# Loads behind the first K issued by GpSimd, one packet per engine and load, in an attention decode kernel

## The chip, the cores and the metric

The kernel runs on one core of a Trainium2 chip. Its engines are TensorE (PE in the profile), VectorE (DVE), ScalarE (ACT), GpSimd (POOL) and SyncE (SP); 16 DMA engines move data between HBM and the on-chip memory of 128 partitions. An engine puts a transfer on a DMA queue with one instruction, and a semaphore tells when it has landed. The metric is the device time of one execution in microseconds (us). Before the change it is 1299.59 us, the median of three runs (1299.52 to 1299.6).

## The reference

One decode step: attention of one query over a cache of 8192 keys, for 2 batches and 32 heads of size 128, times a gate that a small MLP computes, plus the input. Everything is fp32.

```python
x = A_x                                   # (2, 1, 512)
xn = _layernorm(x, axis=-1)
q = (xn @ wq).reshape(B, Sq, H, Dh) ...   # to (2, 32, 1, 128)
scores = jnp.einsum("bhqd,bhkd->bhqk", q, k_cache) * (Dh ** -0.5)
p = _softmax(scores, axis=-1)
o = jnp.einsum("bhqk,bhkd->bhqd", p, v_cache)
s = o ... @ wo                            # (4096, 512)
y = _layernorm(xn); h = _gelu(y @ w1 + b1)
g = _silu(h @ w2 + b2)
return x + s * g
```

The two caches have 2 x 32 x 8192 x 128 elements each, 268 MB each. With the weights the kernel reads 559 MB, each byte once.

## The kernel before

**Tiling.** A unit of work is two heads of one batch, so there are N = 32 units. For each unit the K cache is one load of 128 partitions with 64 KB each (partitions 0 to 63 hold one head, 64 to 127 the other; a partition holds 128 keys of 128 elements), and so is the V cache. On chip there are two buffers for K, `kb[0]` and `kb[1]`, used in turn, and one for V, `vb`. The first and last K and the last V are loaded in two halves of 32 KB per partition.

**Start-up.** `vb` first holds the MLP's weights and small tiles, and `kb[0]` holds wq. SyncE issues w1, w2, the two biases, wq and both halves of the first K (unit 0, into `kb[1]`) without a wait. The MLP runs first; then PE multiplies by wq (line 481), ScalarE copies q, and PE and ScalarE spread q over the partitions (lines 494 and 496). K of unit 1 goes into `kb[0]`, so its load waits for PE's last read of wq; V of unit 0 goes into `vb`, so its load waits for the last reader of the MLP's tiles.

**Loop.** For unit n VectorE multiplies K with q in two halves, in place (line 523), sums each half over the 128 elements into the scores (line 530), and takes the maximum (line 534). Its order within unit n is: multiply first half, maximum of unit n-1 across partitions (line 540), multiply second half, sum first half, sum second half, maximum. PE and ScalarE then do the softmax of unit n-1 (lines 546 to 555), PE multiplies with V (line 574), ScalarE copies the result (line 581). A load of K for unit n+2 is issued when VectorE has summed unit n, whose buffer it overwrites; a load of V for unit n is issued when PE has finished with unit n-1, as there is one V buffer. The last V goes in halves into `kb[1]`. In the end wo is loaded into `vb` in five pieces, and PE multiplies the attention output with it (lines 647 and 656).

**Order.** Every operation is recorded first (`Plan.op`) with the tiles that it reads and writes; `Plan.emit` gives each engine its operations in the order of recording and puts before each the semaphore waits that follow from these tiles. An engine works through its list in order, so a load that waits holds back all that stands behind it on the issuing engine. All loads go through the function `load` at line 313; before the change all of them are SyncE's (line 314). GpSimd has no work after the start-up's fills (lines 342 to 346).

Of the kernel before, what the change touches and what calls it, by code (L numbers as in the profile page):

```python
# [21 lines left out]
class Plan:  # L22
# [18 lines left out]
    def op(self, eng, fn, r=(), w=(), over=(), it=None, loop=False, dma=None):  # L41


        o = Op()
        o.eng, o.fn, o.it, o.loop, o.dma, o.tell = eng, fn, it, loop, dma, False
        need = {}

        def after(d, war):
            if d.dma is None and dma is None and d.eng == eng and (eng == "pe" or war):
                return  # L50
            if d.dma is None:
                if need.get(d.eng) is None or need[d.eng].idx < d.idx:
                    need[d.eng] = d
            else:
                k = ("dma", d.dma)
                if need.get(k) is None or need[k].idx < d.idx:
                    need[k] = d

        for k in r:
            if k in self.writer:  # L60
                after(self.writer[k], False)
        for k in list(w) + list(over):
            if k in self.writer:
                after(self.writer[k], False)
            for d in self.readers.get(k, ()):
                after(d, True)
        clock = self.clock[eng]
        need = {k: d for k, d in need.items() if clock.get(k, 0) < d.idx}
        o.deps = [(k, d) for k, d in need.items()
                  if not any(e is not d and e.done.get(k, 0) >= d.idx for e in need.values())]  # L70
        for _, d in o.deps:
            for k, v in d.done.items():
                clock[k] = max(clock.get(k, 0), v)
        own = eng if dma is None else ("dma", dma)
        self.count[own] = o.idx = self.count.get(own, 0) + 1
        o.done = dict(clock)
        o.done[own] = o.idx
        for k in w:
            self.writer[k] = o
            self.readers[k] = []  # L80
        for k in r:
            if k not in w:
                self.readers.setdefault(k, []).append(o)
        self.ops.append(o)
# [80 lines left out]
def decode_kernel(nc, x, kc, vc, wq, wo, w1, b1, w2, b2, out):  # L165
# [31 lines left out]
    op = plan.op  # L197
# [112 lines left out]
    vf = vc.rearrange("b h s d -> (b h s d)").rearrange("(n p j d) -> n p j d", p=P, j=KP, d=DH)  # L310
    M = KP // 2

    def load(dst, src, sem, w, over=()):
        op("sp", lambda: nc.sync.dma_start(dst, src), (), w, over=over, dma=sem)  # L314

    def load_k(n):
        i = (n + 1) % 2
        if n in (0, N - 1):
            for s in range(2):
                load(kbuf[i][:, s * M:(s + 1) * M], kf[n][:, s * M:(s + 1) * M], f"k{i}{s}", [("kb", i, s)])  # L320
            return
        load(kbuf[i], kf[n], f"kb{i}", [("kb", i, s) for s in range(2)])
# [4 lines left out]


    load(w1_sb, w1.rearrange("(p c) f -> p c f", p=P), "w1", ["w1"])
    load(w2_sb, w2.rearrange("f n -> (f n)").rearrange("(p e) -> p e", p=P), "w2", ["w2"])  # L330
    for t, src, k in ((b1_sb, b1, "b1"), (b2_sb, b2, "b2")):
# [166 lines left out]


    PT, PM, PN = (t for t in scratch[:3])  # L500
    load_k(1)

    def load_v(n):
# [192 lines left out]
```

## Time and profile before

| | |
|---|---|
| median of the runs | 1299.59 us |
| span of the profiled execution | 1298.3 us |
| VectorE busy | 1134.7 us (87%) |
| PE busy | 409.4 us (32%) |
| ScalarE busy | 77.6 us (6%) |
| GpSimd busy | 1.4 us |
| DMA packets, bytes, mean rate | 10827, 559.39 MB, 431 GB/s |

The times of runs are of the whole execution on the device; the profiled execution has a span, from its first to its last instruction, which is 1.3 us less than the median of the runs. The profile lists the busy time of each engine, the span in 40 equal slices with the busy share of each engine and of the DMA engines in tenths, the DMA queues with their packets, the chain of work that ended last, and for each group of loads the time from its issue to its landing. The unit of one slice is 32.5 us. The order of time shows one row per instruction or group: its start, its length, engine, line, operation, tiles, and in brackets the idle time before it and what ended it.

### The profile page before, as it was taken

The page shows a single profiled execution, that of the slowest core. Times are in us where ns is not written, and L with a number is a line of the kernel's source. Part 1 is how long each engine was busy: PE and PEld are TensorE (multiplying, and loading weights), DVE is VectorE, ACT ScalarE, POOL GpSimd, SP SyncE. Part 2 cuts the span into 40 slices and gives each one's busy share as a digit, 9 for nine tenths or more (in the row PEclk, how much of TensorE's full clock was granted, in tenths as well). Part 3 has the DMA queues.
Part 4 walks back from the last instruction along what each step waited for, and adds up shares of the span by engine and source line. Part 5 has one row for each costly group of instructions (what it writes and reads, how often), then busy time and mean ns, then how long its engine had stood idle before and what let it go on. Part 6 is the DMA issues. An engine that isn't in the chain of part 4 may idle for free.

```text
span 1298.3 us, 6788 instructions
## 1 busy us (share of the span) xinstructions
PE 409.4 (32%) x2728; PEld 124.5 (10%) x2728; DVE 1134.7 (87%) x276; ACT 77.6 (6%) x250; POOL 1.4 (0%) x8
## 2 busy tenths in 40 slices
PE   5502333212333311333321333321333321333337
PEld 1100011000101000101100101000101100001103
DVE  3599989888889988889988888988888988888991
ACT  1100000000000000000000000000000000000000
POOL 0000000000000000000000000000000000000000
PEclk9856666556666556666555666655666655666659
DMA  9999999999999999999999999999999999999998
GB/s 406 445 423 444 424 436 436 426 444 426 440 428 430 440 426 444 424 436 436 426 444 426 440 428 434 438 424 444 426 434 436 426 444 426 440 428 434 423 436 360
DMA packets 10827, 559.39 MB, mean 431 GB/s; under 512 B 1208, under 2 KB 1216, under 8 KB 1476
## 3 DMA queue, kind: packets, MB, share of 16 engines
q1 hardware_dynamic: 10816, 559.30, 99.7%
q8 instruction: 4, 0.07, 0.0%
q14 instruction: 3, 0.02, 0.0%
q10 hardware_dynamic: 4, 0.00, 0.0%
HBM read 559.30 MB, written 0.00 MB: 431 GB/s over the span
## 4 chain that ended last, share of the span: by engine, by line
DMA 73%; PE 25%; DVE 1%; issue 0%; ACT 0%; SPq 0%; DVEq 0%
DMA vb<-in_A_v_cache_dram 71%; PE po L574 22%; DMA vb<-in_A_wo_dram 2%; PE s L409 1%; PE po L481 1%; PE s L451 0%; PE s L411 0%; PE acc L656 0%; DVE vb L417 0%; ACT L430 0%; DVE vb L355 0%; PE s L458 0%; SPq L314 0%; DVE vb L366 0%; DVE vb L443 0%
## 5 line engine op out<-in xcount | busy, mean ns | idle before, releaser
L523 DVE TENSOR_TENSOR kb<-kb,Q 128x8192 f32<-128x8192 f32 x64 | 555.6, 8681 | 106.3 <-DMA kb<-in_A_k_cache_dram 97.1
L530 DVE TENSOR_REDUCE sc<-kb 128x64 f32<-128x8192 f32 x64 | 552.3, 8666 | 0.0
L574 PE MATMUL po<-vb,PZ 128*8 128x512 f32 x1984 | 287.3, 744 | 296.4 <-DMA vb<-in_A_v_cache_dram 296.4
L546 PE MATMUL s<-nm,srow 1*128 1x2 f32 x64 | 18.4, 355 | 365.2 <-DVE nm L540 365.2
L574 PEld LDWEIGHTS po<-vb,PZ 128*8 128x8 f32 x1984 | 57.5, 104 | 500.2 <-issue 497.5
L537 PE MATMUL s<-ident,mx 128*1 128x128 f32 x32 | 11.8, 369 | 182.6 <-DVE mx L534 182.6
L546 PEld LDWEIGHTS s<-nm,srow 1*128 1x128 f32 x64 | 15.7, 302 | 374.5 <-DVE nm L540 374.5
L581 ACT COPY o<-po 128x512 f32<-128x512 f32 x32 | 18.7, 585 | 542.9 <-PE po L574 542.9
L547 ACT COPY bias<-s 128x2 f32<-128x2 f32 x32 | 5.1, 160 | 612.9 <-PE s L546 612.9
L583 PE MATMUL s<-mod,o 128*128 128x2 f32 x256 | 33.6, 253 | 22.1 <-ACT o L581 22.1
L583 PEld LDWEIGHTS s<-mod,o 128*128 128x128 f32 x256 | 31.1, 191 | 51.3 <-ACT o L581 51.3
L551 ACT ACTIVATE PZ<-sc,bias 64x128 f32<-64x128 f32 x64 | 25.5, 399 | 1.8
L537 PEld LDWEIGHTS s<-ident,mx 128*1 128x1 f32 x32 | 2.5, 79 | 186.1 <-DVE mx L534 155.5
L589 DVE TENSOR_TENSOR Z<-blk,s 128x8 f32 (+1 forms) x32 | 5.2, 163 | 12.4 <-PE s L583 12.4
L417 DVE COPY vb<-vb 2x384 f32<-2x384 f32 x4 | 1.8, 500 | 15.1 <-ACT vb L413 15.1
L551 ACT ACTIVATION_READ_ACCUMULATOR PZ<-sc,bias 64x1 f32 x64 | 11.8, 185 | 0.0
L409 PE MATMUL s<-vb 128*2 128x512 f32 (+1 forms) x24 | 11.7, 637 | 0.3 <-ACT vb L374 0.3
L665 DVE TENSOR_TENSOR gate<-acc,gate 128x128 f32<-128x128 f32 x1 | 0.3, 292 | 13.0 <-PE acc L656 13.0
L534 DVE TENSOR_REDUCE mx<-sc 128x1 f32<-128x128 f32 x32 | 9.2, 286 | 1.1
L555 ACT ACTIVATE ZR<-half,rs 128x8 f32 (+1 forms) x32 | 9.6, 301 | 4.1
L574 PE MATMUL po<-kb,PZ 128*8 128x512 f32 x64 | 8.7, 705 | 1.4 <-ACT PZ L551 1.4
L540 DVE TENSOR_REDUCE nm<-s 1x2 f32<-1x128 f32 x32 | 8.7, 272 | 0.3 <-PE s L537 0.3
(88 smaller groups left out, 83.8 us busy)
## 6 DMA issues: line engine op xcount, KB each, us to landing
kb<-in_A_k_cache_dram SPq DMA_DIRECT2D x4, 4096.0 KB, 43.3
kb<-in_A_v_cache_dram SPq DMA_DIRECT2D x2, 4096.0 KB, 40.5
vb<-in_B_w_dram SPq DMA_DIRECT2D x2, 2752.0 KB, 12.4
vb<-in_A_wo_dram SPq DMA_DIRECT2D x1, 4096.0 KB, 19.8
vb<-in_A_wo_dram SPq DMA_DIRECT2D x1, 2048.0 KB, 24.4
vb<-in_A_wo_dram SPq DMA_DIRECT2D x1, 1280.0 KB, 27.0
vb<-in_A_wo_dram SPq DMA_DIRECT2D x1, 512.0 KB, 27.7
vb<-in_A_v_cache_dram SPq DMA_DIRECT2D x31, 29.2
```

The lines of the kernel that those rows point to most:

```text
L409: pe(lambda f=f, w=w, ph=ph, c=c: matmul(ph[:B, :w], yT[:, c, :], w1_sb[:, c, f:f + w], start=(c == 0), stop=False), ["yT", "w1"], [k])
L481: pe(lambda i=i, c=c, wv=wv, a=a, j=j, hd=hd: matmul(PO[R * j:R * j + NQ * B, :].rearrange("m (h d) -> m h d", d=DH), xnT[:, c, a:a + NQ * ...
L523: vector(n, n, lambda n: nc.vector.tensor_tensor(out=k, in0=k, in1=cols(Q, n * DH, DH).unsqueeze(1).to_broadcast([P, M, DH]), op=ALU.mult) ...
L530: vector(n, n, lambda n: nc.vector.tensor_reduce(out=SC[:, s * M:(s + 1) * M], in_=k, axis=AX.X, op=ALU.add), [("kb", i, s)], [("sc", s)])
L534: vector(n, n, lambda n: nc.vector.tensor_reduce(out=MX, in_=SC, axis=AX.X, op=ALU.max), [("sc", 0), ("sc", 1)], ["mx"])
L537: pe(lambda i: transpose(PM[:1, :P], MX, ident), ["mx", "ident"], ["s1"], it=n, loop=n > 0)
L546: pe(lambda i: matmul(PN[:, :U], srow, NM, start=True, stop=True), ["srow", "nm"], ["s2"], **one)
L551: act(lambda i, r=r, s=s: nc.scalar.activation(PZ[r, :, s, :], sc[r], AF.Exp, bias=BIAS[r, s:s + 1], scale=SCALE, accum_out=RS[r]), ["bias ...
L555: act(lambda i: nc.scalar.activation(cols(ZR, i * UP - UP, UP), half, AF.Copy, scale=RS), ["half"] + [("rs", s) for s in range(U)], [("ZR" ...
L574: pe(lambda i, t=t, j=j, v=v: matmul(PO[R * j:R * j + U * JW, :], PZ[:, t].rearrange("p s j -> p (s j)"), v[:, t * JW:(t + 1) * JW, :].rea ...
L581: act(lambda i: nc.scalar.copy(O4, PO), ["po"], ["o4"], **one)
L583: pe(lambda i, k=k: matmul(PT[:, :U], O4[:, k * DH:(k + 1) * DH], mod[:, k:U * JW:JW], start=(k == 0), stop=(k == JW - 1)), ["o4", "mod"], ...
```

## The change

The function `load` gets a switch. It is off for the loads of the start-up (w1, w2, the biases, wq, both halves of the first K), which SyncE issues as before, and is turned on before the load of K for unit 1. [...] Waits, buffers, semaphores and the order of the loads among themselves are as before. The output is still stored by SyncE.

```diff
+    stream = [False]
+
     def load(dst, src, sem, w, over=()):
-        op("sp", lambda: nc.sync.dma_start(dst, src), (), w, over=over, dma=sem)
+        if stream[0]:
+            op("pool", lambda: nc.gpsimd.dma_start(dst, src, single_packet=True), (), w, over=over, dma=sem)
+        else:
+            op("sp", lambda: nc.sync.dma_start(dst, src), (), w, over=over, dma=sem)
...
     PT, PM, PN = (t for t in scratch[:3])
+    stream[0] = True
     load_k(1)
```

## The prediction

> **What bounds the kernel now.** I read first the engine totals and the DMA lines of the page, then the chain that ended last, then the order of time around the first issue that the change moves.
>
> ```profile
> span 1298.3 us, 6788 instructions
> DVE  3599989888889988889988888988888988888991
> DMA  9999999999999999999999999999999999999998
> DMA packets 10827, 559.39 MB, mean 431 GB/s; under 512 B 1208, under 2 KB 1216, under 8 KB 1476
> q1 hardware_dynamic: 10816, 559.30, 99.7%
> DMA 73%; PE 25%; DVE 1%; issue 0%; ACT 0%; SPq 0%; DVEq 0%
> kb<-in_A_k_cache_dram SPq DMA_DIRECT2D x30, 42.6
> vb<-in_A_v_cache_dram SPq DMA_DIRECT2D x31, 29.2
> ```
>
> The 16 DMA engines are busy from end to end, all on one queue (q1, SyncE's), and the chain is a transfer of V, PE's product with it, the next transfer of V. VectorE is nine tenths busy in the middle, so it has little room to catch up. The chain's period gives the pace of the loop:
>
> ```profile
> 45.66 49.55 DMA vb<-in_A_v_cache_dram
> 95.33 9.45 PE po L574 x64
> 104.79 29.11 DMA vb<-in_A_v_cache_dram
> 134.03 8.87 PE po L574 x64
> 142.92 29.69 DMA vb<-in_A_v_cache_dram
> 172.73 10.00 PE po L574 x64
> ...
> 1217.67 9.77 PE po L574 x64
> ```
>
> From 134.03 to 1217.67 are 28 rounds of 38.70 us, and one K and one V of 8.389 MB each in 38.70 us are 433.5 GB/s: 19.35 us for a load. A V takes 29.2 us from issue to landing, so it waits 9.8 us behind the K before it; a K (42.6) waits 23 us. What happens between an issue and its first byte is covered by these 9.8 and 23 us, as long as the queue is never empty. The time is set by the bytes and by any gap in the DMA.
>
> **The place where the change acts.** SyncE has put w1, w2, wq and both halves of the first K (K0) on its queue by 3.7 us. The next load, K1, must wait for PE's last read of wq. Here are the start-up's issues and landings, each landing row being the time since its issue, and then VectorE's and SyncE's order of time.
>
> ```profile
> L314 SPq DMA_DIRECT2D vb<-in_B_w_dram x1: 393/393/393, 0.7 to 0.7; - x1
> DMA to landing us min/median/max: 9.4/9.4/9.4
> ...
> L314 SPq DMA_DIRECT2D kb<-in_A_k_cache_dram x2: 457/466/474, 2.8 to 3.3; - x2
> DMA to landing us min/median/max: 43.9/48.5/53.1
> ```
>
> ```profile
> 45.28 0.33 SPq L314 DMA_DIRECT2D kb<-in_A_k_cache_dram  x1
> 45.66 0.43 SPq L314 DMA_DIRECT2D vb<-in_A_v_cache_dram  x1
> 47.74 17.38 DVE L523 TENSOR_TENSOR kb<-kb,Q 128x8192 f32<-128x8192 f32 x2 [8.24 <-ACT Q L496]
> 65.03 17.27 DVE L530 TENSOR_REDUCE sc<-kb 128x64 f32<-128x8192 f32 x2
> 82.33 0.33 SPq L314 DMA_DIRECT2D kb<-in_A_k_cache_dram  x1
> 83.20 8.69 DVE L523 TENSOR_TENSOR kb<-kb,Q 128x8192 f32<-128x8192 f32 x1 [0.58 <-issue]
> 93.47 0.40 ACT L551 ACTIVATE PZ<-sc,bias 64x128 f32<-64x128 f32 x1
> 95.33 9.40 PE L574 MATMUL po<-vb,PZ 128*8 128x512 f32 x64 [2.61 <-DMA vb<-in_A_v_cache_dram]
> 104.79 0.33 SPq L314 DMA_DIRECT2D vb<-in_A_v_cache_dram  x1
> 117.90 0.33 SPq L314 DMA_DIRECT2D kb<-in_A_k_cache_dram  x1
> 118.29 8.69 DVE L523 TENSOR_TENSOR kb<-kb,Q 128x8192 f32<-128x8192 f32 x1
> ```
>
> K0's first half lands at 2.8 + 43.9 = 46.7 us, its second at 3.3 + 53.1 = 56.4, V0 at 95.2. VectorE multiplies the first half at once and meets the second half just as it lands (65.1 − 8.7 = 56.4). So when K1 is issued at 45.28, practically the whole second half of K0, 9.7 us of transfer, is still to move, and VectorE needs it next. Today this is harmless: one queue serves in order. K2, which overwrites K0, is issued at 82.33, and V0 keeps the engines busy until 95.2: 13 us in hand.
>
> **The change part by part.** *What is issued where.* SyncE loses 70 issues (K1 to K31, all V, five pieces of wo); it keeps the seven loads ahead of them and the output's store. GpSimd gets the 70 in the same order with the same waits. Its last instruction before them is a memset of PZ that ends at 2.2 us, so nothing else stands behind its waits, and nobody waits for SyncE's emptier queue.
>
> ```profile
> 1.86 0.31 POOL L346 MEMSET PZ<- 128x256 f32 x1
> ```
>
> *Cost of an issue.* No row shows a load issued by GpSimd. SyncE's take 0.33 to 0.43 us. The transfer into idle engines is w1: 2752 KB are 2.818 MB, 6.5 us at 433.5 GB/s, and it landed after 9.4, so 2.9 us are fixed. I let GpSimd cost between 0.4 us less (nothing for its issue) and 2.9 us more (the fixed part doubled) per load, and take 1 us, nearer the lower end since most of the 2.9 us must lie where the issuer plays no part, at the engines and the landing. In the loop this is hidden behind the 9.8 and 23 us; if that cover is gone, it costs 1 us for each empty queue. [...] At the end the five pieces of wo are issued together:
>
> ```profile
> vb<-in_A_wo_dram SPq DMA_DIRECT2D x1, 4096.0 KB, 19.8
> vb<-in_A_wo_dram SPq DMA_DIRECT2D x1, 256.0 KB, 27.9
> ```
>
> The first has 19.8 − 9.7 = 10 us of cover, the last far more than five issues of at most 3.3 us. Nothing there.
>
> *One packet per engine and load.* The page counts 10816 packets on q1 for 559.30 MB, 51.7 KB each: a packet is now one partition's row (64 KB, or 32 KB in a half). Afterwards an engine's eight rows of a load (128 rows over 16 engines) are one packet. What eight row ends cost today I bound by landings: half a K took 9.7 us in eight short rows, a V or K 19.35 us in eight long ones. Twice 9.7 is 19.4: at most 0.05 to 0.2 us per load for eight row ends. The moved bytes are 64 such loads (31 K, 32 V, wo): times seven eighths, between 0 and 11 us to gain. I take 0, since the difference is no larger than the rounding of the landings. A loss there is not excluded by a row either; I give it the same 0.
>
> *Two queues at 45 to 95 us.* This is the term that matters. K0's second half lies on SyncE's queue as eight packets per engine of 1.2 us each. K1 arrives at 45.3 to 48.2 us on another queue, as one packet per engine of 19.35 us, V0 behind it as another. No row of before has two data queues at work, so the end of K0 lies between 56.4 (its queue goes first) and 95.2 (it goes last; the sum of bytes is the same, so then all three are in at 95.2). I suppose that an engine takes one packet from each queue in turn. Then, after one or two packets of K0, come K1's 19.35 us, one packet of K0, V0's 19.35 us, and only then the other five or six packets: K0 ends at 95.2. The trace's packet sizes put it near the late end: only two packets stand against eight. [...]
>
> The sum, from there. VectorE multiplies K0's second half from 95.2 instead of 56.4 and sums both halves; K2's issue comes 82.33 − 56.4 = 25.9 us after, at 121.1. The engines have been empty since 95.2. K2 lands at 121.1 + 2.9 + 19.35 + 1 = 144.4. V1 waits for PE's product with V0, which waits for the softmax: the second exponential ends at 93.9, that is 11.5 us after K2's issue, the product takes 9.4 and little else, so V1 is issued some 21.3 us after K2, at 142.4, too late to follow K2 without a gap. It lands at 142.4 + 2.9 + 19.35 + 1 = 165.7, where it landed at 104.79 + 29.11 = 133.9. The shift is 31.8 us. Is the queue fed from there on? K3 is issued 117.90 − 82.33 = 35.6 us after K2, at 156.7, before V1 ends. V2: VectorE starts on K2 at 118.29 − 83.20 = 35.1 us after K1, at 157.1; the softmax is through 10.7 us later, the product at 177.3, while K3 moves until about 184. So DMA is the bound again and the 31.8 us stay to the end, because VectorE, although it needs only some 35 us per round, cannot make bytes move faster. Span 1298.3 + 31.8 = 1330.1. The runs' median is 1299.59, 1.3 us over this span: 1331.4, say 1331 us, 2.4% slower.
>
> **The rivals.**
>
> *Row by row in turn.* The one packet is not kept together: an engine alternates a 1.2 us row of K0 with a 2.4 us row of K1. Then K0 ends at 46.7 + 8 × 3.6 = 75.5, K2 is issued at 101.4, V1 at 122.7 and lands at 122.7 + 23.3 = 146.0: 12.1 us late, 1311.7 us. This is also the rival in which the change does not do what it says.
>
> *No harm: queue order holds.* K0 is served first, or K1 starts only when K0 is through. Then all is covered, 1299.6 us. [...]
>
> [...]
>
> *Faster.* The row ends cost their upper bound or half of it, and the queues don't collide: 0.1 us × 64 = 6 us saved, 1293.2. It wins from 0.04 us per load on. Against it: the halves show nothing measurable.
>
> *Worse than the forecast.* Instruction fetches share the engines:
>
> ```profile
> q8 instruction: 4, 0.07, 0.0%
> q14 instruction: 3, 0.02, 0.0%
> ```
>
> Behind a packet of 19.35 us instead of 2.4 a late fetch in the last 30 us could add up to 10 us (half-load packets of 9.7 us there) to the 1331.
>
> **How the numbers follow.** Forecast 0.52, its own range 1326 to 1337 (the issue's bounds, and an issue or two later or earlier); worse 0.06; row by row 0.08; GpSimd held 0.06; no harm 0.14; faster 0.14. About 0.2%, 2.6 us, is what a measurement of this kernel can tell from no change. Faster 0.14, same 0.14, slower 0.72. For eight in ten I reach from 1295, which holds part of the faster case and the one without harm, to 1338.
>
> **What would show it.** Right: a new queue with nearly all bytes; K1 and V0 landed before K0's second half; VectorE idle at line 529 (the multiply) from 56 to about 95 us for a K transfer; a hole in the DMA row of some 27 us from 95 to 123 us; rounds of 38.7 us before and after. Wrong: a K0 that lands at 56 us; rounds other than 38.70 us, which would mean that the packet or GpSimd's issue acts in the loop; holes in the DMA row later on.

## The result and the profile after

The changed kernel takes 1304.72 us (median of 5 runs, 1302.25 to 1305.45) against 1299.55 us of the kernel before, measured beside it: ratio 1.0034 (95% interval 1.0023 to 1.0045). It is slower, by 0.34% or some 4.4 to 5.2 us, where 31 us were forecast. The profiled execution has a span of 1303.4 us, 5.1 us over the span before.

The changed kernel's page first: totals, DMA queues, the chain that ended last, and the group of V's issues (columns: busy us, mean ns of one, idle time before them and what ended it).

```profile
span 1303.4 us, 6788 instructions
DMA packets 10763, 559.39 MB, mean 429 GB/s; under 512 B 1208, under 2 KB 1216, under 8 KB 1412
q0 software_dynamic: 10016, 536.88, 95.3%
q1 hardware_dynamic: 736, 22.43, 4.0%
DMA 65%; PE 23%; issue 5%; DVE 5%; another core or an unknown queue 1%; ACT 0%; POOL 0%; DVEq 0%
L317 POOL DMA_DIRECT2D vb<-in_A_v_cache_dram x31 | 16.4, 528 | 906.5 <-PE po L580 906.5
```

Nearly all bytes are now on a new queue, q0, GpSimd's. An issue takes 0.53 us there, against SyncE's 0.33 to 0.43. And 536.88 MB in 10016 packets are 53.6 KB each: the records still count every row of 64 or 32 KB as a packet, though the load asks for one packet.

The order of time where the issuing engine changes, in the changed kernel (start, length, engine, line; in brackets the idle time before and what ended it):

```profile
47.06 0.67 POOL L317 DMA_DIRECT2D kb<-in_A_k_cache_dram  x1 [44.89 <-PE po L486]
47.73 0.53 POOL L317 DMA_DIRECT2D vb<-in_A_v_cache_dram  x1
49.24 8.69 DVE L529 TENSOR_TENSOR kb<-kb,Q 128x8192 f32<-128x8192 f32 x1 [8.24 <-ACT Q L501]
68.35 8.69 DVE L529 TENSOR_TENSOR kb<-kb,Q 128x8192 f32<-128x8192 f32 x1 [10.42 <-DMA kb<-in_A_k_cache_dram]
76.96 17.27 DVE L536 TENSOR_REDUCE sc<-kb 128x64 f32<-128x8192 f32 x2
94.52 0.53 POOL L317 DMA_DIRECT2D kb<-in_A_k_cache_dram  x1 [46.27 <-DVE sc L536]
105.93 8.51 PE L580 MATMUL po<-vb,PZ 128*8 128x512 f32 x64 [1.29 <-ACT PZ L557]
114.78 0.53 POOL L317 DMA_DIRECT2D vb<-in_A_v_cache_dram  x1 [19.72 <-PE po L580]
```

VectorE waits 10.4 us for K0's second half before it can multiply it at 68.35. Before, it took both halves without a pause. So K2 is issued at 94.52 instead of 82.33, and V1 at 114.78 instead of 104.79. The landings, from the rows of these three lines (times since the issue):

```profile
L319 SPq DMA_DIRECT2D kb<-in_A_k_cache_dram x1: 581/581/581, 3.2 to 3.2; - x1
DMA to landing us min/median/max: 65.1/65.1/65.1
...
L317 POOL DMA_DIRECT2D kb<-in_A_k_cache_dram x1: 528/528/528, 94.5 to 94.5; - x1
DMA to landing us min/median/max: 22.8/22.8/22.8
...
L317 POOL DMA_DIRECT2D vb<-in_A_v_cache_dram x1: 527/527/527, 114.8 to 114.8; - x1
DMA to landing us min/median/max: 22.4/22.4/22.4
```

K0's second half lands at 3.2 + 65.1 = 68.3 us (56.4 before), K2 at 94.5 + 22.8 = 117.3 (82.33 + 32.2 = 114.5 before, by the view of transfers shown next), V1 at 114.8 + 22.4 = 137.2 (133.9 before): 11.9, 2.8 and 3.3 us late. V0 landed at 94.9, just as K2 was issued, so here the engines ran empty. The view of transfers from 40 to 130 us, in slices of 2.25 us, shows it. The kernel before:

```profile
GB/s 415 379 437 466 451 437 495 466 470 466 466 437 408 408 350 350 437 437 466 466 437 477 437 466 437 437 437 408 379 437 350 437 466 437 437 466 466 466 437 466
DMA packets 774, 39.34 MB, mean 437 GB/s; under 512 B 80, under 2 KB 80, under 8 KB 80
...
kb<-in_A_k_cache_dram SPq DMA_DIRECT2D x3, 32.2
```

The changed kernel:

```profile
GB/s 400 393 451 437 510 408 626 189 542 510 422 466 437 466 291 379 408 437 466 466 466 437 437 58 360 117 466 466 466 466 466 466 437 350 146 466 466 466 466 466
DMA packets 745, 37.44 MB, mean 416 GB/s; under 512 B 80, under 2 KB 80, under 8 KB 80
```

The rate falls at two places, 58, 360, 117 around 95 us (ahead of K2) and 350, 146 around 117 us (ahead of V1). Single slices swing: a 64 KB row takes 2.42 us in the records, longer than a slice. Over the whole window 1.90 MB fewer move, which at 433.5 GB/s are 4.4 us; in the packet records the rows of V1 end on average 4.2 us later than before.

From there the loop is as before: PE's products with V start at 176.47 and, 28 rounds later, at 1260.25, 38.71 us a round. The last rows to compare are the order of time at the end (first V30's product, then the first product with wo, then the last one). Before:

```profile
1256.45 9.11 PE L574 MATMUL po<-vb,PZ 128*8 128x512 f32 x64 [13.47 <-DMA vb<-in_A_v_cache_dram]
1285.50 3.66 PE L647 MATMUL wide<-vb,on 128*17 128x512 f32 x32 [0.47 <-DMA vb<-in_A_wo_dram]
1293.49 1.31 PE L656 MATMUL acc<-vb,on 128*17 128x128 f32 x40 [1.15 <-DMA vb<-in_A_wo_dram]
```

After:

```profile
1260.25 9.90 PE L580 MATMUL po<-vb,PZ 128*8 128x512 f32 x64 [13.47 <-DMA vb<-in_A_v_cache_dram]
1290.65 3.65 PE L653 MATMUL wide<-vb,on 128*17 128x512 f32 x32 [0.93 <-DMA vb<-in_A_wo_dram]
1298.65 1.32 PE L662 MATMUL acc<-vb,on 128*17 128x128 f32 x40 [1.16 <-DMA vb<-in_A_wo_dram]
```

V30's product starts 3.80 us late: that is the start-up's loss. The last product starts 5.16 us late: another 1.36 us come in after the loop, between V30 and wo.

### The profile page after: what moved, and what is told of

Its sections match the earlier page's. It is cut to its first block, busy times and chain, and to the rows that moved or that the text cites. A ratio compares the mean times of both kernels' runs of the same rounds, so it can differ in the third digit from the quotient of the medians.

```text
span 1303.4 us, 6788 instructions
## 1 busy us (share of the span) xinstructions
PE 405.7 (31%) x2728; PEld 123.4 (9%) x2728; DVE 1134.7 (87%) x276; ACT 77.6 (6%) x250; POOL 38.5 (3%) x78
## 3 DMA queue, kind: packets, MB, share of 16 engines
q0 software_dynamic: 10016, 536.88, 95.3%
## 4 chain that ended last, share of the span: by engine, by line
DMA 65%; PE 23%; issue 5%; DVE 5%; another core or an unknown queue 1%; ACT 0%; POOL 0%; DVEq 0%
DMA vb<-in_A_v_cache_dram 63%; PE po L580 20%; DVE sc L536 3%; DMA vb<-in_A_wo_dram 2%; DVE kb L529 2%; PE s L414 1%; PE po L486 1%; PE s L456 0%; PE s L416 0%; PE acc L662 0%; DVE vb L422 0%; ACT L435 0%; DVE vb L360 0%; PE s L463 0%
## 5 line engine op out<-in xcount | busy, mean ns | idle before, releaser
L580 PE MATMUL po<-vb,PZ 128*8 128x512 f32 x1984 | 281.3, 731 | 275.1 <-DMA vb<-in_A_v_cache_dram 271.3
L317 POOL DMA_DIRECT2D vb<-in_A_v_cache_dram x31 | 16.4, 528 | 906.5 <-PE po L580 906.5
L589 PE MATMUL s<-mod,o 128*128 128x2 f32 x256 | 33.6, 253 | 22.1 <-ACT o L587 22.1
L317 POOL DMA_DIRECT2D kb<-in_A_k_cache_dram x32 | 17.1, 533 | 289.1 <-DVE sc L536 237.2
```

The costliest lines, as they stand in the source:

```text
L317: op("pool", lambda: nc.gpsimd.dma_start(dst, src, single_packet=True), (), w, over=over, dma=sem)
L580: pe(lambda i, t=t, j=j, v=v: matmul(PO[R * j:R * j + U * JW, :], PZ[:, t].rearrange("p s j -> p (s j)"), v[:, t * JW:(t + 1) * JW, :].rea ...
L589: pe(lambda i, k=k: matmul(PT[:, :U], O4[:, k * DH:(k + 1) * DH], mod[:, k:U * JW:JW], start=(k == 0), stop=(k == JW - 1)), ["o4", "mod"], ...
```

## The experiments

The theory after this reading: while K0's second half is on SyncE's queue and K1 on GpSimd's, the DMA engines take *one row of each queue in turn*, whatever the packet flag says. K0's last rows are slowed by K1's twice as long rows, VectorE gets them 12 us late, K2 is issued when the engines have just run empty. Rivals: the flag does something to the order; it is GpSimd's software queue that is slow, at its start or in general; the loss is made in the loop.

The packet records of the trace show the order directly. They do not name the engine, but its rows follow each other without a gap, so they can be strung together. One engine of the changed kernel, each row's size in KB and start in us from the start of the span (SyncE's queue as K0, GpSimd's as K1):

```
K0 32@44.9  K0 32@46.1  K0 32@47.3  K0 32@48.5  K0 32@49.7
K1 64@50.9  K0 32@53.4  K1 64@54.6  K0 32@57.0  K1 64@58.2
K0 32@60.6  K1 64@61.8  K0 32@64.3  K1 64@65.5  K1 64@67.9
```

From K1's first row on, each 1.2 us row of K0 has a 2.4 us row of K1 ahead of it. And K1 joins late, 3.8 us after its issue at 47.06 (50.85 on the first engine, 52.68 on the last). By then 2 to 4 rows of K0 are left per engine. With four: 50.9 + 4 × 3.63 = 65.5. The landing comes 2.8 us later still, at 68.3. The records have one packet of 4 bytes per engine behind each load, and this packet too waits for its turn: on this engine it comes at 67.89, behind one more row of K1, and the landing is seen 0.4 us after it. In the kernel before it follows the last row at once, at 55.97, and K0 is in at 56.4.

**The changed kernel once more**, beside the next three. No edit.

> The changed kernel once more, as the yardstick for the others. Theory A (handover): when GpSimd's K1 joins the engines, each engine takes one row from each of the two queues in turn, so that K0's second half lands some 10 to 13 us late, K2 is issued late and the queue is empty for 2 to 4 us near 95 and 115 us; rounds of 38.70 us after that. Expected 1302 to 1305.5 us, the second half of K0 landing at 66 to 72 us. Theory B (cost of each load): GpSimd's issue or the packet costs a little at every load; then the rounds are longer than 38.70 us. Theory C (the tail): part of the loss, 1.4 us in the trace at hand, comes behind the last V, from chance positions of the engines; then this part changes sign or size from one profile to the next.

1304.44 us (1301.89 to 1307.75, 6 runs), 1.0036 (1.0024 to 1.0048). K0's second half is met at 68.48, K2 issued at 94.66. The loss is the same, from the same place.

**Without the flag.** GpSimd issues as in the change, the row packets are left as they come.

```diff
-            op("pool", lambda: nc.gpsimd.dma_start(dst, src, single_packet=True), (), w, over=over, dma=sem)
+            op("pool", lambda: nc.gpsimd.dma_start(dst, src), (), w, over=over, dma=sem)
```

> Only single_packet is taken away; GpSimd issues the same loads. Theory A: the rows alternate with or without it, so the time is that of the changed kernel within 0.1% (1302 to 1305.5 us), and K0's second half lands at 66 to 72 us. If the packet does hold rows together in part, the second half lands at least 2 us earlier without it and the time falls by 2 us or more. Theory B with the packet as the cost: the rounds change by 0.05 us or more.

1305.63 us (1302.3 to 1307.32, 5 runs), 1.0041 (1.0029 to 1.0054). GpSimd's queue on its page:

```profile
q0 software_dynamic: 10016, 536.88, 95.2%
```

The second half of K0 in its order of time:

```profile
68.57 8.69 DVE L529 TENSOR_TENSOR kb<-kb,Q 128x8192 f32<-128x8192 f32 x1 [11.13 <-DMA kb<-in_A_k_cache_dram]
```

The same number of packets, the same lateness (68.57 against 68.35 and 68.48), the same time within the intervals. In its packet records the rows alternate in the same way. So the rows that an engine moves for a load do not form one packet, as the change meant them to: the flag has no effect that can be measured here, and this half of the change does nothing.

**All loads on GpSimd's queue.** The switch is on from the first load, so no old rows are left on SyncE's queue when K1 comes.

```diff
-    stream = [False]
+    stream = [True]
```

> All loads from the first on are GpSimd's, so there is one data queue throughout and no handover. Theory A: K0's second half lands 9.7 us behind its first, the queue is never empty between 50 and 1250 us, and the loss is only what the start comes later: 1300 to 1303 us, with the shift already there at the first landing of w1 (up to 3 us). Theory B: a loss of some 4 us at the last product with V that is not there at the first, because it grows with the loads.

1300.49 us (1300.33 to 1300.63, 11 runs), 1.0006 (0.9998 to 1.0015). Its one data queue, from the page:

```profile
q0 software_dynamic: 10800, 559.30, 99.6%
```

Its order of time:

```profile
50.09 17.30 DVE L529 TENSOR_TENSOR kb<-kb,Q 128x8192 f32<-128x8192 f32 x2 [8.24 <-ACT Q L501]
84.87 0.53 POOL L317 DMA_DIRECT2D kb<-in_A_k_cache_dram  x1 [35.88 <-DVE sc L536]
```

VectorE takes both halves in one go, K2 is issued 11 us before V0 is in (96.2), and the loss is gone but for 0.8 us. A ratio of 1 lies within the interval, yet each of the 11 runs lies above each of the 23 of the kernel before beside it (1300.33 against 1299.91 at the nearest). So it isn't GpSimd's issue in the loop, nor its queue, nor the flag, that costs the 5 us. Its loop starts 0.9 us later (V1's product at 134.97 against 134.03) and ends as much later. All of that is there at the first load: w1's first row moves at 2.63 us instead of 1.76, because GpSimd issues it at 1.26 instead of 0.73 and its first row moves 1.37 us after the issue instead of 1.03.

**K1 in halves.** The handover to GpSimd stays where the change has it, but K1's rows are 32 KB, as K0's are.

```diff
-        if n in (0, N - 1):
+        if n in (0, 1, N - 1):
```

> K1 is loaded in two halves of 32 KB per partition, both by GpSimd, all else as in the change. Theory A: a row of K0 then alternates with a row of 1.2 instead of 2.4 us, K0's second half lands at 61 to 65 us instead of 68, K2 is issued before V0 has landed, and the queue is never empty: 1299.4 to 1301.5 us. If engines share by whole loads or by bytes, or if the loss lies in the loop, the time stays at 1302 to 1305.5 us.

1299.74 us (1299.48 to 1301.08, 11 runs), 1.0003 (0.9994 to 1.0012). Its order of time:

```profile
62.38 8.69 DVE L529 TENSOR_TENSOR kb<-kb,Q 128x8192 f32<-128x8192 f32 x1 [5.39 <-DMA kb<-in_A_k_cache_dram]
88.56 0.53 POOL L317 DMA_DIRECT2D kb<-in_A_k_cache_dram  x1 [40.73 <-DVE sc L536]
```

One engine's packet records show one K0 row and one K1 row in turn, now of equal length:

```
K0 32@47.4  K0 32@48.6  K0 32@49.8  K1 32@51.0  K0 32@52.2  K1 32@53.4
K0 32@54.6  K1 32@55.9  K0 32@57.1  K1 32@58.3  K0 32@59.5  K1 32@60.7
```

K0's second half is still late, 62.4 instead of 56.4, but 6 us instead of 12. K2 is issued at 88.56, 6.6 us before V0 has landed (95.2), and nothing is lost at the end of the profiled execution (three of the 11 runs are some 1 us longer). So a late K0 costs nothing by itself; the price begins where K2 comes too late for the queue. Where exactly no run shows: K0 6 us late costs nothing, 12 us late it costs 3.8. The 13 us in hand that the prediction read were too many. V0's last rows end at 92.7 to 94.5 in the changed kernel's records, ahead of its landing, and K2's first row moves 1.2 us after its issue. By these rows K2 has to be issued by about 91.5 us, which leaves some 9 us of cover (an estimate).

**K1 by ScalarE, all else by SyncE.** From the kernel before, without GpSimd and without the flag: only K1 moves, to ScalarE's hardware queue.

```diff
+    op("act", lambda: nc.scalar.dma_start(kbuf[0], kf[1]), (), [("kb", 0, s) for s in range(2)], dma="kb0a")
...
-    load_k(1)
```

> The kernel before, with one load moved: K1 is issued by ScalarE on its own queue, right behind PE's last read of wq; all others stay with SyncE, nothing is GpSimd's. Theory A (rows taken in turn from any two queues): K1's rows start about 2 us after the issue, seven rows of K0 per engine are left then, 7 times 1.2 + 2.4 us, so K0's second half lands at 71 to 75 us, K2 is issued at 97 to 101 us into an empty queue, and the time is 1306 to 1311 us, worse than the change. If the collision were a matter of GpSimd's software queue, K0 lands at 56 us and the time is 1299.6 us.

1306.83 us (1305.88 to 1307.3, 5 runs), 1.0055 (1.0041 to 1.0069), against 1299.68 beside it. Its queues, from the page:

```profile
q1 hardware_dynamic: 10672, 550.91, 97.8%
q10 hardware_dynamic: 148, 8.39, 1.5%
```

Its order of time:

```profile
46.17 0.37 ACTq L486 DMA_DIRECT2D kb<-in_A_k_cache_dram  x1
70.91 8.69 DVE L523 TENSOR_TENSOR kb<-kb,Q 128x8192 f32<-128x8192 f32 x1 [13.18 <-DMA kb<-in_A_k_cache_dram]
96.82 0.33 SPq L314 DMA_DIRECT2D kb<-in_A_k_cache_dram  x1
```

One single load on a second queue, 1.5% of the DMA time, is enough to make the kernel slower by as much as the whole change and more. The collision needs no queue of GpSimd's: SyncE's and ScalarE's do the same. Nor is K1 the first load on ScalarE's queue, which had carried the 4 KB of x at 0.9 us. K1's first row moves 3.5 us after its issue (49.66), not the 2 us that were expected.

**The biases' loads by GpSimd ahead of K1.** Is the late joining of K1 (some 4 to 5 us) the cost of a first load on GpSimd's queue? Then two small loads on that queue in the start-up would take it away; K1 would join earlier and K0 end still later. The loads of b1 and b2 move behind the fill of PZ, to GpSimd.

```diff
-    for t, src, k in ((b1_sb, b1, "b1"), (b2_sb, b2, "b2")):
-        load(t.rearrange("o (k e) -> o k e", k=16), src.rearrange("(o k e) -> o k e", o=1, k=16), k, [k])
...
+    stream[0] = True
+    for t, src, k in ((b1_sb, b1, "b1"), (b2_sb, b2, "b2")):
+        load(t.rearrange("o (k e) -> o k e", k=16), src.rearrange("(o k e) -> o k e", o=1, k=16), k, [k])
+    stream[0] = False
```

> As the change, but the two small biases b1 and b2 are also loaded by GpSimd, at 2 us, so that K1 is no longer its first load. In the changed kernel K1's first row moves 4 to 5 us after its issue, K2's (into an empty queue) about 2 us after. If the difference is a cost of GpSimd's first load, K1 joins some 2 us earlier here, meets one or two rows of K0 more per engine, K0's second half lands 1 to 3 us later than 68.5 us, and the time rises by as much, to 1305 to 1308 us. If the 4 to 5 us are not of the first load, K0 lands at 67 to 69.5 us and the time is that of the changed kernel.

1307.65 us (1304.87 to 1310.04, 5 runs), 1.0062 (1.0048 to 1.0075). Its order of time:

```profile
44.95 0.56 POOL L317 DMA_DIRECT2D kb<-in_A_k_cache_dram  x1 [41.70 <-PE po L488]
70.88 8.69 DVE L531 TENSOR_TENSOR kb<-kb,Q 128x8192 f32<-128x8192 f32 x1 [15.04 <-DMA kb<-in_A_k_cache_dram]
```

It is slower than the change, but not for the reason that was tried. K1's issue came 2.1 us earlier in this execution (44.95 against 47.06: PE was through with wq earlier), and its first rows moved at 48.72 to 49.98, which is 3.8 to 5.0 us after the issue, where the changed kernel has 3.8 to 5.6. (Into empty engines K2 needs 1.2 us there, not 2 as the expectation says.) The delay isn't that of a first load. An earlier issue simply met more of K0, 4 or 5 rows on most engines instead of 2 to 4, and K0 ended 2.5 us later. The time lay where the theory put it and yet the theory falls: the trace decides, not the total.

**A second handover, at wo.** K1 in halves as above, which loses nothing, and the five pieces of wo go back to SyncE's queue while the last V's second half is on GpSimd's.

```diff
+    stream[0] = False
```

(ahead of the loads of wo, beside the edit of the kernel with K1 in halves)

> The kernel with K1 in halves, in which the first handover costs nothing, and wo's five pieces issued by SyncE: a second handover, with the last half of V still on GpSimd's queue. Theory A: from 1268 us on a row of V's last half alternates with a row of wo; the half lands some 8 to 10 us later than 1279.6 us, PE's last product and all that follows it shift with it, since the weights wo, which now come early, can't be used before: 1306 to 1310 us. If queues were served in the order of issue, 1299.7 us as without it.

1304.35 us (1303.51 to 1305.14, 6 runs), 1.0035 (1.0023 to 1.0047). Its order of time:

```profile
1267.03 2.23 SPq L319 DMA_DIRECT2D vb<-in_A_wo_dram  x5
1272.18 5.56 PE L580 MATMUL po<-kb,PZ 128*8 128x512 f32 x32 [1.38 <-ACT PZ L557]
1282.84 5.32 PE L580 MATMUL po<-kb,PZ 128*8 128x512 f32 x32 [5.10 <-DMA kb<-in_A_v_cache_dram]
1293.50 5.38 PE L654 MATMUL wide<-vb,on 128*17 128x512 f32 x48
```

In the kernel with K1 in halves, without this handover, PE takes both halves of V in one go:

```profile
1271.09 8.78 PE L580 MATMUL po<-kb,PZ 128*8 128x512 f32 x64 [1.38 <-ACT PZ L557]
```

A handover at another place costs again, through another wait. The last half of V lands at 1282.8, against 1275.6 without the handover (issued at 1233.19, landed 42.4 us later): 7.2 us late, of which 1.1 come from its own later issue (1234.28). The 1279.6 us of the expectation are not that landing, they are about where PE's product ends (1279.87). wo's first row moved 3.7 us after the issue (1270.72), when two to four rows of V were left per engine. PE waits 5.1 us in the middle of its product and ends it 8.3 us later, at 1288.16. The span grows by only 5.1 us, since the 48 products with wo (line 654), which elsewhere run in pieces as wo lands, now follow without any wait for a transfer: the tail has become PE's.

The runs side by side, each from its profiled execution; shifts are against the kernel before (K2 issued at 82.33, V1 at 104.79, V30's product at 1256.45, span 1298.3).

| kernel | K2 issued | V1 issued | V30's product, shift | span, shift | the rest, behind the loop |
|---|---|---|---|---|---|
| K1 in halves | 88.56 | 109.31 | -0.1 | -0.1 | 0.0 |
| all on GpSimd | 84.87 | 105.17 | 0.9 | 0.9 | 0.0 |
| changed | 94.52 | 114.78 | 3.8 | 5.1 | 1.3 |
| changed, again | 94.66 | 115.97 | 4.5 | 5.4 | 0.9 |
| without the flag | 94.75 | 116.26 | 5.3 | 6.2 | 0.9 |
| K1 by ScalarE | 96.82 | 116.96 | 6.1 | 6.4 | 0.3 |
| biases by GpSimd | 97.05 | 118.05 | 6.7 | 7.4 | 0.7 |
| wo by SyncE too | 88.58 | 110.08 | 1.0 | 5.0 | 4.0 |

Where K2 is issued some 6 us or more before V0 is in (88.6 against about 95 us), the loop is on time to within 1 us. Issued at 94.5 it is too late already. From there the loss follows V1's issue more closely than K2's: three kernels with K2 at 94.52 to 94.75 lose 3.8, 4.5 and 5.3 us, and their V1 is issued at 114.78, 115.97 and 116.26, because PE's product with V0, for which V1 waits, took 8.5, 9.6 and 9.8 us in these executions. So the engines run empty twice, ahead of K2 and ahead of V1, and PE has a share in the second. The 0.3 to 1.3 us behind the loop (last row apart) appear only in the kernels whose queue ran empty. The packet records suggest why: after the empty stretch the 16 engines start together and stay together (they end V30's last row within 0.98 us in the changed kernel, 1.89 us in the one before), and a 16 KB instruction fetch of 1.0 us that falls on one of them near 1284 us then makes that engine the last (its first 16 KB row of wo moves at 1290.1 us, those of the others at 1287.8 to 1288.8). In the kernel before, the fetch comes at 1279.6 us and its engine's first 16 KB row moves at 1284.8, among the others' 1283.1 to 1285.0: there it is lost in the spread. This is argued from the records and was not tested by a run of its own.

## Why the prediction was wrong in size and right in direction

- *What bounds the kernel.* Right: rounds of 38.71 us after, 38.70 before. GpSimd's issues cost nothing in the loop, as said: 0.53 us instead of 0.33 lies inside the 9.8 and 23 us of waiting behind the queue.
- *Cost of an issue by GpSimd.* K2, sent into empty engines, landed 22.8 us after its issue. The working had 2.9 + 19.35 + 1 = 23.3: the extra was 0.5 us, not 1. Beside loads that SyncE itself sent into empty engines (K1 by ScalarE: K2 23.3, V1 22.9 us) even that does not show: GpSimd's K2 and V1 in the changed kernel, its repeat and the kernel without the flag took 22.1 to 23.6.
- *Row ends, taken as 0.* Right in the sum: the rounds didn't get shorter. A 32 KB row takes 1.213 us in the records and a 64 KB row 2.418, so about 8 ns of a row do not grow with its bytes. Seven row ends in each of 64 loads are 64 × 7 × 8 ns = 3.6 us at most, and none of it was saved, because rows are still moved one by one.
- *Two queues at 45 to 95 us.* The place is right, and so is each link behind it: K0's second half late, VectorE idle for a K transfer, K2 late, the engines empty, V1 late, the loss carried through the loop to the end. **The step that failed is "I suppose that an engine takes one packet from each queue in turn", with a load's eight rows as that one packet.** In the records an engine took one row of each queue in turn, with the flag or without it (K1 at 50.9, K0 at 53.4, K1 at 54.6, K0 at 57.0 us on one engine of the changed kernel). So K0's second half was in at 68.3 and not at 95.2. No run shows a load's eight rows as one turn, on which the 95.2 rested; with the 32 and 64 KB rows of this kernel the records show a switch after every single row.
- *The rival "row by row in turn"* is what happened, and it was given 0.08. Its condition was stated rightly, and also that then the change does not do what it says. Its size was wrong as well: it let K1 join at once, at 46.7, with all eight rows of K0 left, and had K0 in at 75.5 and a loss of 12.1 us. K1 joined at 50.9 to 52.7, with two to four rows left, and one more row of K1 stood ahead of the packet that closes the load, which the rival left out. So K0 was in at 68.3 instead of 75.5, and the loss was 3.3 us at V1's landing and 3.8 us at V30's product instead of 12.1.
- *What the sum had no term for:* some 1.3 us behind the loop, whose cause stays open.
- *The other rivals.* "No harm" fails, for the queues do collide: K0's second half was in at 68.3 us instead of 56.4. The 0.06 for a GpSimd held up by VectorE fails too: the issues at 47.06 and 47.73 took 0.67 and 0.53 us, K1's rows began to move at 50.85 in the middle of VectorE's multiply (49.24 to 57.93), and the 31 issues of V have a mean of 528 ns with VectorE busy 87% of the time. "Faster" fails by the rounds. "Worse by instruction fetches" names what the packet records suggest for the tail, with some ten times the size; no run tests it.
- *The range* held the time only by luck, because it reached down to the cases without loss. The forecast's own range, 1326 to 1337, did not.

The chances were put wrongly in one respect that could have been seen. The change's own words suggested the most harmful rule, and it got 0.52; the kernel's page before already counted a row as a packet, and the rule by which a row takes a turn got 0.08.

## What to carry to other kernels

The stream of loads that moved to another queue here did not wait for what was still on the old one: the engines moved a 1.2 us row of K0 and a 2.4 us row of K1 in turn, and the load that was needed next came 12 us late. A kernel that moves a stream while loads are still on the old queue should look for this in its records. Two ways out were run: one queue for all loads (1300.49 us, 0.8 us lost, all of it at the first load), and a newcomer's rows of the length of the old ones (K1 in halves: 6 us late instead of 12, and nothing lost). To let the old queue run out first follows from the same reading but was not run. Then ask not how late the load is but whether the next issue still comes before the queue is empty; past that point the later issues were paid for (3.8 us with V1 issued at 114.78, 6.7 with 118.05).

## What the runs showed of the hardware that was not expected

- A load on a queue that was idle moved its first row 3.5 to 4.1 us after its issue while the engines worked for another queue, for example GpSimd 47.06 to 50.85 and 44.95 to 48.72, ScalarE 46.17 to 49.66, SyncE 1267.03 to 1270.72. Into empty engines it was 1.2 us from GpSimd (K2, 94.52 to 95.76) and 1.0 from SyncE (K2 of the kernel with K1 by ScalarE, 96.82 to 97.78). The longer delay was much the same on the queue that the page calls software (3.8 us in both cases) and on those that it calls hardware (3.5 and 3.7), and with the biases ahead on GpSimd's queue it was no shorter (3.8). Its cause no run here shows.
- The 4-byte packet behind a load's last row took its turn like a row. With a second queue at work it came one whole row of that queue later: 65.47 to 67.89 us behind a 64 KB row, and 60.71 to 61.92 behind a 32 KB row with K1 in halves.
- `single_packet` on rows of 32 to 64 KB changed neither the number of packets (10016 both ways) nor the order of rows nor the time.
- The changed kernel's runs spread over some 3 to 6 us (1301.89 to 1307.75), those of the kernel before over 0.5. PE's progress in the start-up varies by about 2 us, as the times of K1's issue show (44.95 to 47.06 in the kernels with a handover). In the kernel before, K1, issued at 45.28, stood behind K0 on one queue and moved its first row at 54.1; now an earlier K1 meets more of K0 and makes the end later (issued at 44.95 instead of 47.06, K0 was met at 70.88 instead of 68.35). That this explains the whole spread was not shown.
- No kernel tried is faster than the one before. The best, K1 in halves, is not to be told from it, and all loads by GpSimd is 0.8 us behind it in the medians.
